# Hash attention and a gated feed-forward on one core: score masks of two blocks on quarters of TensorE's rows, score blocks and products with v by turns

## The chip, the core and the metric

The kernel runs on one core of a Trainium2 chip. The metric is the device time of one launch in microseconds (us). A core has TensorE (PE: matrix products, with its weight loads on their own row, PEld), VectorE (DVE), ScalarE (ACT), GpSimd (POOL) and SyncE (SP), which here only issues transfers. Each engine works through its own instructions in the order of the program and waits at an instruction until the semaphores that it names have been raised.

## The reference

```python
batch, n_heads, seq, head_dim = (4, 8, 768, 64)
q_bits = (np.einsum('bhsd,dk->bhsk', q, proj) > 0)      # 6 bits of each row
k_bits = (np.einsum('bhsd,dk->bhsk', k, proj) > 0)
mask = q_bucket[:, :, :, None] == k_bucket[:, :, None, :]
scores = scale * np.matmul(q, k.transpose(0, 1, 3, 2))
scores = np.where(mask, scores, -1000000000.0)
attn = softmax(scores)
x = np.matmul(attn, v)                # then (B,H,S,D) -> (B*S, H*D) = (3072, 512)
h = x @ w_in                          # 512 -> 2048
out = (h * erf(softplus(h))) @ w_out  # 2048 -> 512
```

A query attends only to the keys that have the same six bits.

## The kernel before, in words

The 32 heads are taken in 16 pairs. Two heads of 64 dimensions lie on the 128 partitions, one on the lower and one on the upper half (`ab` is 0 or 1 in the code). A pair has four groups n = 4 i to 4 i + 3: two halves of the queries (384 columns each), and for each half two groups of keys, of three blocks (c = 0, 1, 2) of 128 keys. So a half has 6 blocks, a pair 12, and attention 192.

`score` (line 730) computes one block, keys down and queries across, for both heads at once. Each head has its own bank of PSUM; a block takes one buffer `st` of two banks, and there are three such buffers. It is made in two steps. The mask step (source "b") is one bf16 product per head of the signs of the bits: `both` holds them, 64 rows per head, of which 7 are used (six bits and a constant) and the others are zero. It adds a very large negative number unless all bits agree. The plain step adds k times q in f32; an f32 product shows as two matmuls in the profile, so four for the two heads. Both steps use TensorE as two halves of 64 rows by 128 columns (the "64\*128" of a row in the profile).

ScalarE then takes the exponential of the block (`exponential`, line 772) into `e_even` or `e_odd`, one for each parity of the half; `e_odd` lies in the tile named `area`. VectorE adds up the exponentials of a pair (`sum_keys`, line 818). `weigh` (line 830) multiplies a group's three blocks with v; the two heads use two halves of TensorE's columns ("128\*64"), and the result of a half gathers in one bank, `av`. ScalarE copies it away (`leave`, line 895). The divisor is a product of the sums with ones on quarters of the columns ("128\*32", `divisor`, line 874); from there it goes through DRAM, is inverted on VectorE and comes back (`spread` to `normalise`, lines 914 to 957).

The bits of a pair are prepared ahead: TensorE multiplies q and k with the projection (`bits_of`, line 1033, "128\*32"), ScalarE takes the sign into `sg` (line 1042), VectorE scales it (line 1052), GpSimd writes it to DRAM (`leave_bits`, line 1062) and reads it back to its place in one of the two mask buffers (`place_bits`, line 1071, two transfers per pair). Pair 0's bits are made in place, without DRAM; its buffer is cleared afterwards (`clean`, line 1080).

Beside attention, the weights of the feed-forward are fetched by GpSimd and converted on ScalarE and VectorE (lines 651 to 727), 32 pieces.

TensorE's order in attention is a list written by hand (`order`): all 12 blocks of a pair (four entries "score"), then the products with v of all 12 (four entries "weigh"), then the bits of the pair after next and the divisor of the pair before. `pe(...)` gives each entry a cost and what it comes after; a score block must wait until the block that had its buffer three places ago has been taken by ScalarE. `arrange` then plays all engines forward with these costs and so sets the order of the other engines' instructions. The feed-forward follows (line 1493 on): TensorE begins it with products of the first tokens and w_in, for which VectorE has made sums of weights and tokens (lines 983 and 511) at the end of attention, and VectorE adds the first results up (line 1516).

Of the kernel before, what the change touches and what calls it, by code (L numbers as in the profile page):

```python
# [63 lines left out]
P = 128  # L64
# [288 lines left out]
def kernel(  # L353
# [11 lines left out]
    nc = tc.nc  # L365
# [241 lines left out]
    def attention():  # L607
        NS = NPAIR * 4
        with (
# [121 lines left out]
            def score(n, c, parts=((0, "b"), (1, ""))):  # L731

                i, half, g = n // 4, n // 2 % 2, n % 2
                d = pairs[i]
                cols = slice(half * HS, (half + 1) * HS)
                keys = slice((g * GC + c) * P, (g * GC + c + 1) * P)
                if ("st", n, c) in d:
                    parts = ((1, "b"),)
                else:
                    d["st", n, c] = big("st")  # L740
                st = d["st", n, c]
                for part, src in parts:
                    for ab in range(2):
                        rows = slice(ab * D, ab * D + D)
                        nc.tensor.matmul(  # L745
                            out=st[:, ab, 0:HS],
                            lhsT=d["k" + src][rows, keys],
                            rhs=d["q" + src][rows, cols],
                            start=(part == 0),
                            stop=(part == 1),  # L750
                        )

            def plain(n, c):
# [63 lines left out]
                        into, one, two = last_sums[:, 0, :, :], s[:, 0, 0, :, :], s[:, 0, 1, :, :]  # L817
                nc.vector.tensor_tensor(out=into, in0=one, in1=two, op=ALU.add)  # L818

            def weigh(n):  # L820
                half, g = n // 2 % 2, n % 2
                d = pairs[n // 4]
                if g == 0:
                    d["av", half] = bank("av") if half else psum_v.tile([P, 512], F32, name="av", tag="av")
                w = HS + 1 - half
                for c in range(GC):
                    e = block(n, c)
                    for ab in range(2):
                        rows = slice(ab * D, ab * D + D)
                        nc.tensor.matmul(  # L830
                            out=d["av", half][rows, 0:w],
                            lhsT=d["v"][:, g * GC + c, rows],
                            rhs=e[:, ab, 0:w],
                            start=(g == 0 and c == 0),
                            stop=(g == 1 and c == GC - 1),
                        )
# [227 lines left out]
            def place_bits(i):  # L1064

                d = pairs[i]
                bd = d.pop("bd")
                for n, what in enumerate(("qb", "kb")):
                    d[what] = both[i % 2][:, n, :]
                for ab in range(2):  # L1070
                    nc.gpsimd.dma_start(
                        out=both[i % 2][ab * D : ab * D + NBIT + 1, :, :].rearrange(
                            "r w (h c) -> r (w h) c", h=2
                        ),
                        in_=bd[:, ab, 0 : NBIT + 1, :].rearrange("n r c -> r n c"),
                    )

            def clean(n):

# [2 lines left out]
            chain = []  # L1082
            order = []
            PACE = 18
            for i in range(NPAIR):
                for k in range(4):
                    order.append(("score", 4 * i + k))
                    if i == 0 and k == 1:
                        order.append(("bits", 1))
                order += [("weigh", 4 * i + k) for k in range(4)]  # L1090
                if i + 2 < NPAIR:
                    order.append(("bits", i + 2))
                if 0 < i < NPAIR - 1:
                    order.append(("divisor", i - 1))
                if i == NPAIR - 2:
                    order.append(("divisor", i))
            slots = []
            for what, n in order:
                free = slots[-3] if len(slots) >= 3 else ()
                if what == "score":  # L1100
                    i = n // 4
                    after = (("place_bits", i),)
                    for c in range(GC):
                        free = slots[-3] if len(slots) >= 3 else ()
                        pe(score, (n, c), 0.82 if n or c == 2 else 0.17, after + free)
                        slots.append((("exponential", n, c),))
                elif what == "bits":
                    pe(bits_of, (n,), 0.80, (("start_pair", n),) + free)
                    slots.append((("sign_of", n),))
                elif what == "divisor":  # L1110
                    if n != NPAIR - 3:
                        free = ()
                        slots[-1] += (("keep_divisor", n),)
                    else:
                        slots.append((("keep_divisor", n),))
                    pe(divisor, (n,), 0.72, (("sum_keys", n, last_sum(n)),) + free)
                else:
                    h = n // 2
                    after = (("exponential", n, GC - 1),)
                    if n % 2 == 0:  # L1120
                        after += (("leave", h - 2), ("leave_plain", (h - 2) // 2))
                    pe(weigh, (n,), 2.0, after)
            sums_after = {}
            for i in range(NPAIR):
                for k, (_, blocks_) in enumerate(sum_steps(i)):
# [1543 lines left out]
```

## Time and profile before

| what | us |
|---|---|
| median of three timed runs | 866.1 (865.98 to 866.86) |
| the profiled execution, as timed | 866.67 |
| its span, first to last instruction | 864.9 |
| TensorE busy | 858.7 |
| VectorE busy | 728.2 |
| ScalarE busy | 636.5 |
| first feed-forward product begins | 312.84 |

The profile is of one execution; times in it count from its first instruction. In the timeline a row has the start, how long until the last of its instructions ended, engine, line, operation, what it writes and reads, the shape (for TensorE rows by columns of the array that are in use, then partitions by elements that stream), and how many instructions were merged into the row. Matmuls of TensorE overlap, so that the distance from start to start says what one costs, and the duration does not. In the rows that group instructions, the number behind the bar is busy time, and then the mean of one in ns.

### The profile page before, as it was taken

How to read it: one execution, taken by the hardware profiler on the slowest of the kernel's cores; microseconds unless marked ns; L12 is line 12 of the kernel's file. 1: busy time of each engine (PE TensorE's matmuls, PEld its weight loads, DVE VectorE, ACT ScalarE, POOL GpSimd, SP SyncE). 2: the span in 40 equal slices, each digit the busy share in tenths (PEclk: the TensorE clock that was granted, in tenths of full speed). 3: DMA queues.
4: the chain of work that ended last, by engine and by line, in shares of the span. 5: the costliest groups of instructions: out<-in, count | busy, mean ns of one | idle time of the engine just before them, and what ended most of it. 6: DMA issues, size and time to landing. Idle time of an engine off the chain costs nothing.

```text
span 864.9 us, 15750 instructions
## 1 busy us (share of the span) xinstructions
PE 858.7 (99%) x6184; PEld 672.6 (78%) x6184; DVE 728.2 (84%) x987; ACT 636.5 (74%) x890; POOL 179.5 (21%) x262
## 2 busy tenths in 40 slices
PE   9999999999999999999999999999999999999997
PEld 5444545444454468899999999999999999999997
DVE  5999999999999799778677999798879777967992
ACT  6888888888888759984689455876785768667840
POOL 1111111111111000233242334331321441110000
PEclk9999999999999999999999999999999999999999
DMA  9566876655663336497565658846667667555222
GB/s 224 155 177 196 212 213 166 192 149 149 185 170 111 102 130 220 144 357 270 184 167 181 222 174 249 280 150 217 176 226 267 208 219 203 207 184 176 75 69 70
DMA packets 103939, 160.57 MB, mean 186 GB/s; under 512 B 35646, under 2 KB 49006, under 8 KB 102960
## 3 DMA queue, kind: packets, MB, share of 16 engines
q1 hardware_dynamic: 94288, 126.47, 47.1%
q0 software_dynamic: 9120, 32.55, 11.9%
q8 instruction: 51, 0.84, 0.4%
q10 hardware_dynamic: 448, 0.46, 0.2%
q14 instruction: 32, 0.26, 0.1%
HBM read 125.01 MB, written 30.24 MB: 180 GB/s over the span
## 4 chain that ended last, share of the span: by engine, by line
PE 99%; DVE 1%; ACT 0%; issue 0%
PE M L1730 25%; PE st L745 18%; PE M L2038 18%; PE av L830 15%; PE M L2197 8%; PE X L2197 6%; PE M L1493 6%; PE bits L1033 1%; PE bits L874 1%; PE warm L994 1%; PE X L2038 0%; PE bits L564 0%; PE z_ps L874 0%; DVE h L1897 0%; DVE e L1897 0%; DVE w_out_sb L2123 0%
## 5 line engine op out<-in xcount | busy, mean ns | idle before, releaser
L1890 ACT ACTIVATE w<-w,cq 128x1024 f32<-128x1024 f32 x144 | 162.3, 1145 | 1.8
L745 PE MATMUL st<-q,k 64*128 64x384 f32 x768 | 155.1, 482 | 0.0
L1730 PE MATMUL M<-area,w_in_sb 128*128 128x128 f32 x1120 | 142.8, 275 | 0.0
L1760 DVE TENSOR_TENSOR h<-M,h 128x512 f32<-128x512 f32 x161 | 107.9, 685 | 37.4 <-PE M L1730 35.7
L1730 PEld LDWEIGHTS M<-area,w_in_sb 128*128 128x128 f32 x1120 | 137.2, 192 | 2.3
L1890 ACT ACTIVATE w<-h,cq 128x1024 f32<-128x1024 f32 x96 | 107.9, 1142 | 13.8 <-DVE e L1897 7.4
L2038 PE MATMUL M<-w_out_sb,h 128*128 128x256 f32 x464 | 109.9, 379 | 0.0
L1730 PE MATMUL M<-i,w_in_sb 128*128 128x128 f32 x840 | 107.4, 275 | 0.0
L1730 PEld LDWEIGHTS M<-i,w_in_sb 128*128 128x128 f32 x840 | 103.2, 192 | 1.8
L745 PEld LDWEIGHTS st<-q,k 64*128 64x128 f32 x768 | 68.5, 187 | 36.0 <-issue 34.6
L2038 PEld LDWEIGHTS M<-w_out_sb,h 128*128 128x128 f32 x464 | 83.9, 190 | 9.1
L818 DVE TENSOR_TENSOR area<-area 128x1536 f32<-128x1536 f32 (+1 forms) x46 | 79.1, 1720 | 7.0 <-ACT area L772 5.7
L1882 ACT ACTIVATE e<-h 128x1024 f32<-128x1024 f32 x48 | 50.5, 1053 | 37.2 <-DVE h L1760 30.8
L772 ACT ACTIVATE e_even<-st 128x768 f32<-128x768 f32 x96 | 73.9, 819 | 0.4 <-PE st L745 0.3
L1712 POOL TENSOR_TENSOR i<-area,i 128x128 f32<-128x128 f32 x70 | 41.6, 615 | 151.4 <-PE M L1730 150.6
L772 ACT ACTIVATE area<-st 128x768 f32<-128x768 f32 x90 | 72.7, 811 | 0.3 <-PE st L745 0.3
L1897 DVE SCALAR_TENSOR_TENSOR e<-w,e 128x1024 f32<-128x1024 f32 x48 | 61.3, 1279 | 13.2 <-ACT w L1890 13.1
L1897 DVE SCALAR_TENSOR_TENSOR h<-w,e 128x1024 f32<-128x1024 f32 x48 | 62.2, 1297 | 9.2 <-ACT w L1890 8.6
L830 PE MATMUL av<-e_even,v 128*64 128x385 f32 x384 | 65.7, 490 | 0.0
L745 PE MATMUL st<-both 64*128 64x384 bf16 x384 | 63.0, 323 | 0.2 <-ACT e_even L772 0.2
L830 PE MATMUL av<-area,v 128*64 128x384 f32 x360 | 60.6, 486 | 0.0
L2038 PE MATMUL M<-wt,area 128*128 128x256 f32 x224 | 55.8, 380 | 0.0
(203 smaller groups left out, 1368.8 us busy)
## 6 DMA issues: line engine op xcount, KB each, us to landing
w_in_sb<-wi_P SPq DMA_DIRECT2D x35, 1792.0 KB
raw<-in_w_out_dram POOLq DMA_DIRECT2D x16, 512.0 KB, 4.1
w_in_sb<-wm_M SPq DMA_DIRECT2D x30, 256.0 KB
raw<-in_w_in_dram POOLq DMA_DIRECT2D x14, 512.0 KB, 5.7
v<-in_v_dram SPq DMA_DIRECT2D x32, 192.0 KB
out_dram<-area SPq DMA_DIRECT2D x23, 256.0 KB
q<-in_qkT_dram SPq DMA_DIRECT2D x30, 192.0 KB
k<-in_qkT_dram SPq DMA_DIRECT2D x30, 192.0 KB
```

The costliest lines, as they stand in the source:

```text
L745: nc.tensor.matmul(out=st[:, ab, 0:HS], lhsT=d["k" + src][rows, keys], rhs=d["q" + src][rows, cols], start=(part == 0), stop=(part == 1),)
L772: nc.scalar.activation(out=e[:, :, 0:HS], in_=st[:, :, 0:HS], func=AF.Exp, scale=scale)
L818: nc.vector.tensor_tensor(out=into, in0=one, in1=two, op=ALU.add)
L830: nc.tensor.matmul(out=d["av", half][rows, 0:w], lhsT=d["v"][:, g * GC + c, rows], rhs=e[:, ab, 0:w], start=(g == 0 and c == 0), stop=(g = ...
L1493: nc.tensor.matmul(out=kept[where][:, u, :], lhsT=a[:, kc, f : f + P], rhs=b[:, kc, :], start=(first and u == 0 and kc == 0), stop=(end an ...
L1730: nc.tensor.matmul(out=out_[:, c, :], lhsT=ring[:, W_AT[q], n % 2, c * P : (c + 1) * P], rhs=x, start=((q in ("Q1", "Q5") or q == "Q2" and ...
L1760: nc.vector.tensor_tensor(out=out_, in0=bank_, in1=one, op=ALU.add)
L1882: nc.scalar.activation(out=s, in_=unit(t, q, fl), func=AF.Silu)
L1890: nc.scalar.activation(out=st["q", t, q, fl, j], in_=f, func=func, scale=scale, bias=cq[:, column : column + 1])
L1897: nc.vector.scalar_tensor_tensor(out=unit(t, q, fl) if last else s, in0=st.pop(("q", t, q, fl, j)), scalar=GATE_S[j][1], in1=s, op0=ALU.ad ...
L2038: nc.tensor.matmul(out=where[:, sub, :], lhsT=a[:, j // G, j % G, sub * P : (sub + 1) * P], rhs=b[:, j, :], start=first, stop=end, skip_gr ...
L2197: nc.tensor.matmul(out=where[:, n * P : n * P + P], lhsT=a[:, j, :], rhs=b[:, j, :], start=(q in ("Q1", "Q2") and j == 0), stop=(q in ("Q4 ...
```

## The change

It does five things.

1. A new function `masks` does the mask steps of two blocks together. Each head's bits are now held twice, in rows 0 to 6 and 32 to 38 of its 64; the first block uses the first quarter of TensorE's rows in each half, the second block the second. These are four bf16 matmuls of 32 rows by 128 columns. The plain steps of the two blocks follow. Pair 0 keeps the mask step of `score`.
2. `place_bits` places each head's bits twice: four transfers per pair instead of two.
3. The order on TensorE is made by halves: two score blocks, then two blocks' products with v of the half before, three times in each half. The first half has no products with v, and at the end those of the last half stand alone.
4. `weigh` takes some of a group's blocks at a time.
5. Bits of the pair after next follow the second half of a pair; the divisors of pairs 13 and 14 move behind the first half of pair 15.

```diff
                 if ("st", n, c) in d:
-                    parts = ((1, "b"),)
+                    parts = ((1, "b" if n == 0 and c < 2 else ""),)
...
+            def masks(*two):
+                i, half = two[0][0] // 4, two[0][0] // 2 % 2
+                d = pairs[i]
+                for n, c in two:
+                    d["st", n, c] = big("st")
+                for p, (n, c) in enumerate(two):
+                    keys = slice((n % 2 * GC + c) * P, (n % 2 * GC + c + 1) * P)
+                    for ab in range(2):
+                        rows = slice(ab * D + p * QR, ab * D + (p + 1) * QR)
+                        nc.tensor.matmul(
+                            out=d["st", n, c][:, ab, 0:HS],
+                            lhsT=d["kb"][rows, keys],
+                            rhs=d["qb"][rows, half * HS : (half + 1) * HS],
+                            start=True,
+                            stop=False,
+                        )
...
                 for ab in range(2):
-                    nc.gpsimd.dma_start(
-                        out=both[i % 2][ab * D : ab * D + NBIT + 1, :, :].rearrange(
...
+                    for row in (ab * D, ab * D + QR):
+                        nc.gpsimd.dma_start(
+                            out=both[i % 2][row : row + NBIT + 1, :, :].rearrange(
...
-            for i in range(NPAIR):
-                for k in range(4):
-                    order.append(("score", 4 * i + k))
...
-                order += [("weigh", 4 * i + k) for k in range(4)]
...
+            for h in range(NPAIR * 2 + 1):
+                i, half = divmod(h, 2)
+                scores = [(2 * h + g, c) for g in range(2) for c in range(GC)] if h < 2 * NPAIR else []
+                weighs = [(2 * h - 2 + g, c) for g in range(2) for c in range(GC)] if h else []
+                for k in range(GC):
+                    if scores:
+                        order.append(("masks" if i else "score", scores[2 * k : 2 * k + 2]))
+                    if weighs:
+                        order.append(("weigh", weighs[2 * k : 2 * k + 2]))
+                if h == 0:
+                    order.append(("bits", 1))
+                elif half and i + 2 < NPAIR:
                     order.append(("bits", i + 2))
-                if 0 < i < NPAIR - 1:
+                if half and 0 < i < NPAIR - 2:
                     order.append(("divisor", i - 1))
-                if i == NPAIR - 2:
-                    order.append(("divisor", i))
+                elif h == 2 * NPAIR - 2:
+                    order += [("divisor", i - 2), ("divisor", i - 1)]
...
-                        pe(score, (n, c), 0.82 if n or c == 2 else 0.17, after + free)
...
+                    if what == "masks":
+                        pe(masks, tuple(n), 0.17, after)
+                        for each in n:
+                            pe(score, each, 0.66)
```

In the rows below, a line of the order that stands for one matmul with f32 operands is two in the profile. TensorE before, the end of pair 1 (`both1` has its bits, `st_` and a number is one score buffer in use, `av_478` and `av_501` are the results of its two halves):

```order
L745 LDWEIGHTS both1_157
L745 MATMUL st_462<-both1_157 128x384
L745 MATMUL st_462<-q_204,k_205 128x384 x2
L745 LDWEIGHTS both1_157
L745 MATMUL st_471<-both1_157 128x384
L745 LDWEIGHTS both1_157
L745 MATMUL st_471<-both1_157 128x384
L745 MATMUL st_471<-q_204,k_205 128x384 x2
L830 MATMUL av_478<-e_even_159,v_206 64x385 x12
L830 MATMUL av_501<-area_76,v_206 64x384 x12
L1033 MATMUL bits_535<-q_379,proj_q_68 32x384 x2
```

TensorE now, in the second half of the same pair:

```order
L763 LDWEIGHTS both1_157
L763 MATMUL st_438<-both1_157 128x384
L763 LDWEIGHTS both1_157
L763 MATMUL st_438<-both1_157 128x384
L763 LDWEIGHTS both1_157
L763 MATMUL st_439<-both1_157 128x384
L763 LDWEIGHTS both1_157
L763 MATMUL st_439<-both1_157 128x384
L745 MATMUL st_438<-q_204,k_205 128x384 x2
L745 MATMUL st_439<-q_204,k_205 128x384 x2
L848 MATMUL av_460<-e_even_159,v_206 64x385 x4
L763 LDWEIGHTS both1_157
```

Each block's mask step stood ahead of its plain step; now both masks stand ahead of both plain steps, and four products with v of the half before (`e_even`) follow, ahead of the next masks.

GpSimd before, from the bits of pair 1 on (`bd` is their place in DRAM, `raw` a piece of weights):

```order
L1062 DMA bd_290<-sg_155 128x384
L1080 MEMSET both0_156 128x1536
L651 DMA raw_317<-in_w_in_dram 128x1024
L1071 DMA both1_157<-bd_290 7x4x384 x2
L651 DMA raw_372<-in_w_in_dram 128x1024
L1062 DMA bd_399<-sg_155 128x384
```

GpSimd now, at the same place:

```order
L1080 DMA bd_285<-sg_155 128x384
L651 DMA raw_315<-in_w_in_dram 128x1024
L1090 DMA both1_157<-bd_285 7x4x384 x4
L1099 MEMSET both0_156 128x1536
L1080 DMA bd_354<-sg_155 128x384
L651 DMA raw_383<-in_w_in_dram 128x1024
```

The transfers that place pair 1's bits are four, and the clearing of pair 0's mask buffer has moved from ahead of them to behind them.

More of the change, by code (lines that the diff above doesn't have):

```diff
@@ L818, in sum_keys, with weigh @@
                 nc.vector.tensor_tensor(out=into, in0=one, in1=two, op=ALU.add)
-            def weigh(n):
+            def weigh(n, some=()):
                 half, g = n // 2 % 2, n % 2
                 d = pairs[n // 4]
-                if g == 0:
+                if ("av", half) not in d:
                     d["av", half] = bank("av") if half else psum_v.tile([P, 512], F32, name="av", tag="av")
                 w = HS + 1 - half
-                for c in range(GC):
+                for c in some or (GC - 1,):
                     e = block(n, c)
@@ L1099, in attention @@
                 free = slots[-3] if len(slots) >= 3 else ()
[L1100 to L1104, printed above, removed]
-                        pe(score, (n, c), 0.82 if n or c == 2 else 0.17, after + free)
-                        slots.append((("exponential", n, c),))
+                if what in ("score", "masks"):
+                    after = (("place_bits", n[0][0] // 4),)
+                    for each in n:
+                        after += slots[-3] if len(slots) >= 3 else ()
+                        slots.append((("exponential",) + each,))
+                        if what == "score":
+                            pe(score, each, 0.82 if each[0] or each[1] == 2 else 0.17, after)
+                    if what == "masks":
+                        pe(masks, tuple(n), 0.17, after)
+                        for each in n:
+                            pe(score, each, 0.66)
                 elif what == "bits":
@@ L1117, in attention @@
                 else:
-                    h = n // 2
-                    after = (("exponential", n, GC - 1),)
-                    if n % 2 == 0:
+                    h = n[0][0] // 2
+                    after = (("exponential", 2 * h + 1, GC - 1),)
+                    if n[0] == (2 * h, 0):
                         after += (("leave", h - 2), ("leave_plain", (h - 2) // 2))
-                    pe(weigh, (n,), 2.0, after)
+                    for m, c in n:
+                        if c < GC - 1:
+                            pe(weigh, (m, (c,)), 0.66, after)
+                        else:
+                            pe(weigh, (m,), 0.66, after)
             sums_after = {}
```

11 lines of the change are left out of this document (4 added, 7 removed).

## The prediction

> **What bounds the kernel now.** I read the page first, then the busy time in stretches, then the timeline of TensorE through one pair of heads.
>
> ```profile
> span 864.9 us, 15750 instructions
> ...
> PE 858.7 (99%) x6184; PEld 672.6 (78%) x6184; DVE 728.2 (84%) x987; ACT 636.5 (74%) x890; POOL 179.5 (21%) x262
> ...
> PE 99%; DVE 1%; ACT 0%; issue 0%
> ```
>
> ```profile
> 100.00:200.00 100.00, 100.00 (x718) 48.08 (x716) 95.73 (x127) 83.87 (x147) 14.59 (x26) 1.00 0.66 179
> 200.00:300.00 100.00, 100.00 (x714) 48.34 (x712) 88.86 (x112) 83.91 (x144) 12.90 (x23) 1.00 0.49 137
> ```
>
> TensorE has no idle time in attention (columns: PE, PEld, DVE, ACT, POOL, then the granted clock, 1.00), and the chain that ended last is 99% TensorE. So whatever TensorE spends more or less, the span follows, until another engine has no time left. VectorE is the next candidate, at 95.73 of 100.
>
> But "busy" does not say that TensorE streams all that time. The timeline shows the spacing of starts:
>
> ```profile
> 103.04 0.83 PE L874 MATMUL bits<-area,ones 128*32 128x384 f32 x8
> 103.80 0.34 PE L745 MATMUL st<-both 64*128 64x384 bf16 x2
> 103.97 0.81 PE L745 MATMUL st<-q,k 64*128 64x384 f32 x4
> 104.62 0.33 PE L745 MATMUL st<-both 64*128 64x384 bf16 x2
> ...
> 112.69 0.33 PE L745 MATMUL st<-both 64*128 64x384 bf16 x2
> 112.85 0.81 PE L745 MATMUL st<-q,k 64*128 64x384 f32 x4
> 113.59 4.10 PE L830 MATMUL av<-e_even,v 128*64 128x385 f32 x24
> 117.53 4.04 PE L830 MATMUL av<-area,v 128*64 128x384 f32 x24
> 121.50 0.52 PE L1033 MATMUL bits<-q,proj_q 128*32 128x384 f32 x2
> ...
> 121.84 0.49 PE L1033 MATMUL bits<-q,proj_q 128*32 128x384 f32 x2
> ...
> 122.16 0.83 PE L874 MATMUL bits<-area,ones 128*32 128x384 f32 x8
> 122.92 0.34 PE L745 MATMUL st<-both 64*128 64x384 bf16 x2
> 123.10 0.81 PE L745 MATMUL st<-q,k 64*128 64x384 f32 x4
> 123.74 0.33 PE L745 MATMUL st<-both 64*128 64x384 bf16 x2
> ```
>
> A pair takes 122.92 - 103.80 = 19.12 us. One score block is its mask step (two bf16 matmuls side by side on 64 rows each, 112.85 - 112.69 = 0.16) and its plain step (four f32 matmuls, 0.645 to the next start, as from 103.97 to 104.62): 0.807. Twenty-four matmuls with v take 3.94, so four of them, one block, take about 0.65.
>
> Where the shape of the array changes (the "64*128" of a row: rows by columns), starts come later than the stream asks. From the last plain step to av: 113.59 - 112.85 = 0.74 instead of 0.645, 0.095 too late. From av to bits: 121.50 - 117.53 = 3.97 instead of 24 x 0.161 = 3.87, 0.10. From the sums by ones to a mask: 122.92 - 122.16 = 0.76 instead of two steps of 0.32, some 0.11. From bits to those sums the shape stays 128*32, although the sums wait for VectorE's semaphore, and the spacing stays at 0.32. So the pause goes with the shape and not with the waiting. Behind it the first matmul is also longer, since its weights were not loaded ahead:
>
> ```profile
> L830 PE MATMUL av<-e_even,v x24: 484/486/538, 113.6 to 117.2; 128*64 128x385 f32 x24
> L745 PE MATMUL st<-both x8: 322/323/333, 122.9 to 125.4; 64*128 64x384 bf16 x8
> L745 PE MATMUL st<-q,k x8: 482/482/587, 6.5 to 7.6; 64*128 64x384 f32 x8
> ```
>
> (min/median/max in ns.) That is 0.05 for the first av, 0.01 for the first bf16 mask, and 0.105 for a first f32 plain step; the last row is the one place, at 6.5 us, where plain steps come directly behind another shape.
>
> **The change, part by part.** The sum is against the profiled execution, 866.67 us; the median of the three timed runs is 866.1, 0.6 lower.
>
> *Masks of two blocks at once.* All but pair 0 use it: 180 of 192 blocks, 90 steps instead of 180. If four matmuls on 32 rows each stream side by side as two on 64 rows do, a step still takes 0.16, so 90 x 0.161 = 14.5 us go. The trace has four side by side only on columns (the sums by ones: eight matmuls of 384 columns in 0.83). At worst quarters stream two by two and nothing goes. I take 14.5, since the column quarters do stream together.
>
> *More changes of shape.* Per round (two blocks) TensorE now goes masks, plain, v, masks. There are 31 halves behind the first, with 3 rounds each: 93 steps of v, 90 of them with masks. Before there were 16 stretches of v. So the step from plain to v happens 93 - 16 = 77 times more often, at 0.095 + 0.05: 11.2 us. The step from v directly to a score did not exist; it comes 93 - 14 (bits follow) - 1 (divisors follow half 30) - 1 (feed-forward follows) = 77 times, at 0.10 + 0.01: 8.5 us. Changes around bits and divisors stay as many as before.
>
> *Masks to plain.* This step was free, both being 64*128. Now it goes from 32*128 to 64*128, which no row shows. From below: 0, if only a change of columns or of the full height pauses. From above: the pause 0.095 plus the first plain step's 0.105, 0.20. Every change of shape seen paused by about 0.1, also 128*64 to 128*32, where only the tile got smaller; I take 0.20: 90 x 0.20 = 18.0 us (bounds 0 to 18).
>
> The Trainium skill, "TensorEngine Tiling (Array Packing)", section Tiling Modes, says that changing the tiling mode, and not just the tile, drains TensorE, and it lists 64x128 and 32x128 as different modes. The trace agrees where columns change, with 0.095 us, and no row shows rows alone changing; by the rule alone, weights loaded ahead, the step would cost 90 x 0.095 = 8.6 us, by mine 18.0.
>
> *Pair 1's masks come earlier and their DMAs are twice as many.*
>
> ```profile
> 16.61 0.55 POOL L1062 DMA_DIRECT2D bd<-sg  x1 [14.03 <-DVE sg L1052]
> 23.39 1.14 POOL L1071 DMA_DIRECT2D both<-bd  x2 [3.53 <-DMA bd<-sg]
> both<-bd POOLq DMA_DIRECT2D x30, 21.0 KB, 2.5
> ```
>
> ```profile
> 13.57 0.34 PE L745 MATMUL st<-both 64*128 64x384 bf16 x2
> ...
> 27.21 0.34 PE L745 MATMUL st<-both 64*128 64x384 bf16 x2
> ```
>
> GpSimd cannot issue them before the bits have left, 23.39. Four instead of two, 0.57 each: the fourth starts at 25.1 and lands 2.1 to 2.5 later, at 27.2 to 27.6. Before, TensorE was there at 27.21. Now half 0's v comes between pair 0's later blocks and half 1's goes into pair 1: from 13.57 three rounds of 2 x 0.807 + 0.146 + 1.29 + 0.11 = 3.16, then the bits of pair 2, 0.77: 23.8. It waits 3.6 us (2 to 5), once; behind the waiting mask its whole queue stands. Later pairs have a pair's time for the same: lateness of 1.1 us in the fourth landing is covered by the other pair's 20 us. The clearing of the other mask buffer and a weight fetch move behind or ahead of these issues on GpSimd and cost TensorE nothing there.
>
> *Waits for free score buffers.* A pair of masks needs two of three. The later one is that of the block two back on TensorE, whose plain step ended 0.65 + 0.15 + 1.29 + 0.11 = 2.2 us earlier, and ScalarE needs about 0.2 + 0.82 for it:
>
> ```profile
> L772 ACT ACTIVATE e_even<-st 128x768 f32<-128x768 f32 x90 | 69.6, 819 | 0.4 <-PE st L745 0.3
> ```
>
> 1.2 us to spare hold one other operation of ScalarE (0.7). Cost 0; without that cover some 0.3 a round.
>
> *VectorE and ScalarE* keep their work: 95.73% and 83.87% of 19.12, that is 18.3 and 16.0 us a pair. They stay hidden as long as TensorE needs more than 18.3.
>
> *The end.* The sums of pair 15 now start behind the divisors of pair 13, which stand behind half 30, about 13.5 us ahead of feed-forward (three rounds and six blocks of v).
>
> ```profile
> 293.72 1.50 PE L874 MATMUL z_ps<-area,ones 128*32 128x384 f32 x16
> 312.84 5.45 PE L1493 MATMUL M<-area,w_in_sb 128*128 128x256 f32 x24
> 317.14 0.69 DVE L1594 TENSOR_TENSOR h<-w_in_sb,h 128x512 f32<-128x512 f32 x1
> 318.40 0.69 DVE L1516 TENSOR_TENSOR h<-M,h 128x512 f32<-128x512 f32 x1 [0.57 <-PE M L1493]
> ```
>
> Before it was 312.84 - 293.72 = 19.1 us. So VectorE enters feed-forward up to 5 us later than it did; it had 0.6 to spare at its first addition there, and TensorE's next use of these banks is some microseconds off. I take 0, with 0 to 4.
>
> *Sum:* -14.5 + 11.2 + 8.5 + 18.0 + 3.6 = +26.8. 866.67 + 26.8 = 893.5, and 0.6 less for a median: 893. A pair then takes about 19.12 - 0.97 + 6 x 0.20 + 5 x (0.146 + 0.11) = 20.6 us, and VectorE is at 89%.
>
> **The rivals.**
>
> *Rows alone don't pause* (chance 0.18). The step from masks to plain stays free, weights still loaded under the masks: 18.0 less, 875. For it: plain weights (64 rows) were always loaded under a running mask. Against: every change of shape on record paused. Between the two, pause without the weights' load: 884 (0.06).
>
> *The pause belongs to semaphores, not to shapes* (0.04 with its weaker form). Each pause on record stands where a matmul waits for another engine at a new stage. If that were the cause, the inner rounds, whose v steps mostly wait for nothing, would not pause: -14.5 + 3.6, bounded by VectorE's 18.3 us a pair instead of 17.8 while weights are converted, some +2: 858, faster than before. It decides if v follows plain without 0.095. Against: bits to sums waits and doesn't pause.
>
> *Quarters don't stream together* (0.06). Masks of two blocks take 0.32: 14.5 more, 908. The Trainium skill, "TensorE: Matmul & The Clock Gate", section Part 3, gives 3.07 times for four tiles of 32 rows, not four; by that a step would take 0.21, an estimate of 4 us more than mine. No run here shows it.
>
> *Waits in every round or at feed-forward's start* (0.06). ScalarE's order was planned for rounds of 2.8 us without pauses; if exponentials come behind two other operations, 0.1 to 0.2 us for each of 90 rounds: 902 to 911.
>
> **How the numbers follow.** The forecast, 893, has 0.60; its own range is 888 (stall 2, weights partly ahead) to 899 (stall 5, 4 at the end). The range 873 to 899 takes in the free step from masks to plain and leaves out the faster case, the quarters and the waits, 0.16. A measurement here can tell about 0.2%, 1.7 us, from no change. Faster 0.03 is the semaphore case; same 0.01 is kept for that case with its gain eaten by VectorE; all others are slower, 0.96.
>
> **What the changed profile would show.** Right: a masks step of four bf16 matmuls 0.16 to 0.18 long; 0.25 from its start to the first plain start and a first plain matmul of about 587 ns; v starting 0.74 behind the second plain step; a round of 3.2 us; a wait of TensorE near 24 us that a DMA of both ends. Wrong: plain 0.16 behind the masks with 482 ns throughout (875), v without pause (858), or idle TensorE in each round that ScalarE ends (above 899).

## The result, and the profile after

The changed kernel takes 900.6 us (median of four runs, 897.9 to 901.2) against 866.5 for the kernel before. The ratio is 1.0387, with a 95% interval of 1.0365 to 1.0410. The forecast was 893.0 with a range up to 899: the sign was right, the size 7.6 us short, and the time lies 1.6 us outside the range.

The first lines of the page, for the changed kernel's profiled execution (901.18 us as timed):

```profile
span 899.0 us, 15777 instructions
...
PE 887.6 (99%) x6184; PEld 655.2 (73%) x6184; DVE 730.6 (81%) x987; ACT 628.5 (70%) x890; POOL 197.2 (22%) x292
...
PE 93%; DVE 4%; ACT 1%; DMA 1%; issue 0%; POOL 0%; DVEq 0%
```

The span is 34.1 us longer (899.0 against 864.9). TensorE has as many instructions as before, 6184, but 29 us more busy time. And the chain that ended last has been 99% TensorE; now 7% of it runs over other engines and a DMA. So there are two kinds of loss, and the first product of the feed-forward separates them: it began at 312.84 and now begins at 342.98, 30.1 us later; from there to the end it was 552.0 us and is 556.0.

**The rounds.** TensorE's timeline in the middle of attention (start, duration, engine, line, operation, shape, count):

```profile
102.07 0.34 PE L763 MATMUL st<-both 32*128 32x384 bf16 x4
102.34 1.56 PE L745 MATMUL st<-q,k 64*128 64x384 f32 x8
103.83 1.51 PE L848 MATMUL av<-e_even,v 128*64 128x385 f32 x8
105.28 0.34 PE L763 MATMUL st<-both 32*128 32x384 bf16 x4
...
111.70 0.52 PE L1051 MATMUL bits<-q,proj_q 128*32 128x384 f32 x2
...
132.37 0.52 PE L1051 MATMUL bits<-q,proj_q 128*32 128x384 f32 x2
```

A round is 105.28 - 102.07 = 3.21 us, and a pair, from one set of bits to the next, 132.37 - 111.70 = 20.67. Forecast were 3.2 and 20.6. The masks of two blocks take 0.27 to the next start, and no row of this stretch shows TensorE idle. The durations of single matmuls (minimum, median and maximum in ns) in this same round, plain steps and then products with v:

```profile
L745 PE MATMUL st<-q,k x8: 482/482/587, 102.3 to 103.4; 64*128 64x384 f32 x8
L848 PE MATMUL av<-e_even,v x8: 484/487/538, 103.8 to 104.9; 128*64 128x385 f32 x8
```

587 ns for the first plain matmul and 538 for the first with v are the late weights, 0.105 and 0.05. They come in every round: from 100 to 200 us the mean of the plain matmuls is 508 ns, that is 482 and a quarter of 105, one late matmul in four.

The busy time in stretches (PE, PEld, DVE, ACT, POOL, then the granted clock) shows that no other engine has become the bound: VectorE went from 95.73 to 83.47.

```profile
100.00:200.00 100.00, 100.00 (x662) 38.93 (x660) 83.47 (x109) 75.87 (x134) 17.44 (x31) 1.00 0.60 164
```

**Pair 1's start.** The timeline of TensorE from the bits of pair 2 on (in brackets the idle time ahead of a row and what ended it):

```profile
23.64 0.49 PE L1051 MATMUL bits<-k,proj_q 128*32 128x384 f32 x2
25.78 0.33 PE L763 MATMUL st<-both 32*128 32x384 bf16 x1 [1.64 <-DMA both<-bd]
26.89 0.34 PE L763 MATMUL st<-both 32*128 32x384 bf16 x2 [0.78 <-DMA both<-bd]
27.43 0.49 PE L763 MATMUL st<-both 32*128 32x384 bf16 x1 [0.20 <-DMA both<-bd]
27.85 2.93 PE L745 MATMUL st<-q,k 64*128 64x384 f32 x8
30.71 2.83 PE L848 MATMUL av<-area,v 128*64 128x384 f32 x8
33.47 0.51 PE L763 MATMUL st<-both 32*128 32x384 bf16 x4
33.91 1.56 PE L745 MATMUL st<-q,k 64*128 64x384 f32 x8
```

The wait is there: without it the masks would have begun at 24.06 (the last bits' start, 23.64, and 0.42 to the next shape), and the last of the four begins at 27.43, 3.4 us later. But what follows is new: the eight matmuls of two plain steps take from 27.85 to 30.71, 2.86 us, where 1.49 is usual (102.34 to 103.83), and the products with v 2.76 instead of 1.45. The stretches say why:

```profile
26.00:27.00 1.00, 0.22 (x3) 0.09 (x2) 1.00 (x1) 0.55 (x2) 1.00 (x1) 1.00 0.17 43
27.00:28.00 1.00, 0.80 (x5) 0.25 (x3) 0.97 (x2) 0.00 (x0) 0.59 (x2) 0.55 0.00 0
28.00:30.00 2.00, 2.00 (x8) 1.03 (x8) 1.97 (x3) 0.45 (x1) 0.25 (x1) 0.50 0.14 49
...
33.00:34.00 1.00, 1.00 (x8) 0.20 (x6) 0.97 (x2) 0.00 (x0) 0.15 (x1) 0.53 0.94 354
34.00:36.00 2.00, 2.00 (x12) 0.94 (x14) 0.28 (x1) 1.13 (x2) 0.43 (x1) 1.00 0.77 161
```

The granted clock was halved. If it has only the values 1.00 and 0.50, a mean of 0.55 in the slice from 27 means low for 0.90 of it, and 0.53 in the one from 33 low for 0.94: from 27.10 to 33.94, 6.84 us. TensorE had work from 27.43 on. From there to the plain steps at 33.91 it took 6.48 us, where the same steps in the round above take 3.21 + 0.27 = 3.48: 3.0 us lost, a little less than half, since the eight plain matmuls and the eight with v did not quite double.

The four timed executions bear this out. Three have a mean granted clock of 0.995 and take 900.4 to 901.2 us; one has 1.000 and takes 897.9, that is 2.5 to 3.3 us less, and lies inside the forecast's range. So the wait does not lower the clock in every execution of this kernel.

**The feed-forward's start.** TensorE in the changed kernel:

```profile
342.98 5.45 PE L1525 MATMUL M<-area,w_in_sb 128*128 128x256 f32 x24
348.35 0.84 PE L892 MATMUL X<-area,ones 128*32 128x384 f32 x4
350.28 0.84 PE L892 MATMUL X<-area,ones 128*32 128x384 f32 x4 [1.09 <-DVE area L836]
...
372.16 3.72 PE L1525 MATMUL M<-area,w_in_sb 128*128 128x256 f32 x16 [1.50 <-ACT h L1538]
...
376.30 3.72 PE L1525 MATMUL M<-area,w_in_sb 128*128 128x256 f32 x16 [0.41 <-ACT M L1541]
```

The divisor of pair 15 (`X`, L892) waits for VectorE's sums of that pair; some 22 us on TensorE waits again, for ScalarE's copies of results. In the kernel before, neither place waits:

```profile
318.22 0.85 PE L874 MATMUL X<-area,ones 128*32 128x384 f32 x8
...
338.40 7.17 PE L1493 MATMUL M<-area,w_in_sb 128*128 128x256 f32 x32
```

Compared matmul by matmul with that kernel, each counted from the feed-forward's first product, TensorE is 1.9 us late behind the first of these places, 3.6 behind the second, 4.2 behind the third. VectorE's timeline at that place, first before the change, then after:

```profile
305.81 0.90 DVE L818 TENSOR_TENSOR area<-q,k 128x768 f32<-128x768 f32 x1
```


```profile
329.00 1.76 DVE L836 TENSOR_TENSOR area<-e_even 128x1536 f32<-128x1536 f32 x1 [0.62 <-PE z_ps L892]
...
339.73 0.16 DVE L919 TENSOR_SCALAR ev<-av 128x1 f32<-128x1 f32 x1 [1.38 <-ACT x_last L913]
...
345.30 0.95 DVE L836 TENSOR_TENSOR area<-q,k 128x768 f32<-128x768 f32 x1
```

The sums of pair 15 (L836) begin at 329.00, but the pieces that the second half of that divisor needs begin only at 345.30, 2.3 us behind the feed-forward's first product; before, they began 7.0 us ahead of it. They stand behind the copy of a column of `av` (L919), which waits for ScalarE, behind inversions, and behind sums for the feed-forward.

So the account of the span's 34.1 us has three parts: the forecast's rounds (-14.5 + 11.2 + 8.5 + 18.0 = 23.2; 15 pairs at 20.67 instead of 19.12 are 23.3) and the wait (3.4), a low clock (3.0), and the feed-forward's start (4.0): 33.6. Of the 0.5 left, 0.2 lies ahead of all this: the mask step behind the bits of pair 1 begins at 13.79 instead of 13.57, with TensorE's order still the same. The low clock and the feed-forward's start still needed proof.

### The profile page after: what moved, and what is told of

Read it like the earlier page. It is cut to its first block, busy times and chain, and to the rows that moved or that the text cites. A ratio compares the mean times of both kernels' runs of the same rounds, so it can differ in the third digit from the quotient of the medians.

```text
span 899.0 us, 15777 instructions
## 1 busy us (share of the span) xinstructions
PE 887.6 (99%) x6184; PEld 655.2 (73%) x6184; DVE 730.6 (81%) x987; ACT 628.5 (70%) x890; POOL 197.2 (22%) x292
## 4 chain that ended last, share of the span: by engine, by line
PE 93%; DVE 4%; ACT 1%; DMA 1%; issue 0%; POOL 0%; DVEq 0%
PE M L1762 24%; PE M L2070 17%; PE st L745 15%; PE av L848 15%; PE M L2229 8%; PE X L2229 6%; PE st L763 3%; PE M L1525 2%; PE bits L1051 1%; PE bits L892 1%; DVE area L836 1%; DMA bd<-sg 1%; ACT w L1922 1%; DVE h L1626 1%; PE warm L1012 1%
## 5 line engine op out<-in xcount | busy, mean ns | idle before, releaser
L745 PE MATMUL st<-q,k 64*128 64x384 f32 x768 | 151.5, 511 | 0.0
L745 PEld LDWEIGHTS st<-q,k 64*128 64x128 f32 x768 | 66.7, 187 | 41.7 <-issue 18.3
L836 DVE TENSOR_TENSOR area<-area 128x1536 f32<-128x1536 f32 (+1 forms) x46 | 79.9, 1738 | 13.3 <-ACT area L790 12.7
L790 ACT ACTIVATE area<-st 128x768 f32<-128x768 f32 x90 | 68.4, 808 | 31.3 <-PE st L745 31.2
L848 PE MATMUL av<-e_even,v 128*64 128x385 f32 x384 | 72.7, 499 | 0.0
L848 PE MATMUL av<-area,v 128*64 128x384 f32 x360 | 69.3, 507 | 0.0
L848 PEld LDWEIGHTS av<-e_even,v 128*64 128x64 f32 x384 | 23.3, 136 | 43.4 <-issue 35.8
```

The lines of the kernel that those rows point to most:

```text
L745: nc.tensor.matmul(out=st[:, ab, 0:HS], lhsT=d["k" + src][rows, keys], rhs=d["q" + src][rows, cols], start=(part == 0), stop=(part == 1),)
L790: nc.scalar.activation(out=e[:, :, 0:HS], in_=st[:, :, 0:HS], func=AF.Exp, scale=scale)
L848: nc.tensor.matmul(out=d["av", half][rows, 0:w], lhsT=d["v"][:, g * GC + c, rows], rhs=e[:, ab, 0:w], start=(g == 0 and c == 0), stop=(g = ...
```

## The experiments

The theory: each round costs what the forecast said, the rest is a low clock after idle time, and an order of VectorE that was planned for a shorter round than TensorE has. The rivals stand with each run. "Begins" is the feed-forward's first product, "from there" the time to the end of the span. In these traces the mask step behind the bits of pair 1, up to which TensorE's order is the same in all, begins between 12.95 us (the last row of the table) and 13.79 (the changed kernel), and at 14.76 with half the exponentials; differences of "begins" carry these differences too.

| kernel | median us | ratio to before, 95% | begins | from there |
|---|---|---|---|---|
| before | 866.5 | | 312.8 | 552.0 |
| changed | 900.6 | 1.0387 (1.0365 to 1.0410) | 343.0 | 556.0 |
| turns only | 892.1 | 1.0295 (1.0278 to 1.0312) | 335.9 | 554.1 |
| packed masks only | 905.6 | 1.0453 (1.0436 to 1.0471) | 351.2 | 552.0 |
| the same, half the exponentials | 884.0 | 1.0206 (1.0189 to 1.0223) | 329.2 | 551.9 |
| v blocks ahead | 898.2 | 1.0365 (1.0348 to 1.0382) | 337.0 | 560.5 |
| divisors earlier | 902.2 | 1.0416 (1.0399 to 1.0433) | 342.2 | 558.0 |
| 24 products in the wait | 899.6 | 1.0383 (1.0366 to 1.0400) | 341.6 | 556.1 |
| 14 products in the wait | 898.2 | 1.0372 (1.0354 to 1.0389) | 339.7 | 556.0 |
| true costs | 896.9 | 1.0342 (1.0325 to 1.0359) | 342.4 | 552.7 |
| true costs, v blocks ahead | 892.4 | 1.0301 (1.0279 to 1.0324) | 337.5 | 553.4 |
| turns only, true costs, v ahead | 886.3 | 1.0234 (1.0217 to 1.0251) | 331.2 | 553.1 |

### Turns only

The changed order with each block's own mask step on 64 rows, and two transfers for a pair's bits:

```diff
-                    for row in (ab * D, ab * D + QR):
+                    for row in (ab * D,):
...
-                        order.append(("masks" if i else "score", scores[2 * k : 2 * k + 2]))
+                        order.append(("score", scores[2 * k : 2 * k + 2]))
```

> The new order with each block's own mask step on 64 rows again, and two transfers for a pair's bits. Theory (each change of the array's shape pauses TensorE, rows included): a round is 3.16 us instead of the changed kernel's 3.21, 4.2 us less over 90 rounds, and the wait ahead of pair 1's masks is about 1.3 us shorter: 895 us, or 892 if the low clock behind that wait goes with it. Rival (packing the masks pays and only the turns cost): taking the packing back adds up to 14.5 us to 900.6: 915.

It took 892.1, and the rival's 915 is out. That this is the theory's second figure is in part luck: the low clock did not go, it became shorter, and the feed-forward's start lost 2.0 us where it had lost 4.0, which the theory did not have. The packed masks, with their change of shape, thus cost 8.5 us on top of the turns and save nothing: some 4 of them in the rounds (3.21 for 3.16), the rest by a longer wait, a longer low clock and the feed-forward's start. The timeline of TensorE in this run, and the plain steps' durations:

```profile
101.10 0.34 PE L745 MATMUL st<-both 64*128 64x384 bf16 x2
101.28 0.81 PE L745 MATMUL st<-q,k 64*128 64x384 f32 x4
```

```profile
L745 PE MATMUL st<-q,k x8: 482/482/483, 101.3 to 102.4; 64*128 64x384 f32 x8
```

From masks to plain on the same 64 rows no plain matmul is longer than 483 ns; behind masks on 32 rows the first took 587. The loads of the plain step's weights begin within the row of loads at 101.10 here, beside the masks, and in the changed kernel at 102.34, behind them. So a change of the rows alone keeps the weights' load from going ahead, 0.105, and makes a pause, 0.09: from 101.10 to 101.28 is 0.18, and the changed kernel's step from 102.07 to 102.34 is 0.27. The clock fell here too, after a wait of 2.1 us in which TensorE was idle for 1.55 and 0.18, and for half as long; the stretches:

```profile
25.00:26.00 1.00, 0.76 (x4) 0.51 (x6) 0.94 (x3) 0.88 (x4) 0.57 (x2) 0.92 0.00 0
26.00:29.00 3.00, 3.00 (x12) 1.36 (x10) 2.93 (x5) 1.05 (x2) 1.17 (x3) 0.50 0.10 33
29.00:30.00 1.00, 1.00 (x8) 0.28 (x4) 0.90 (x2) 1.00 (x2) 0.88 (x2) 0.88 0.84 102
```

Low for 0.16 of the first, all of the second and 0.24 of the third: 3.40 us. From the second mask, at 25.57, to the next round's masks, at 30.37, are 4.80 us where 3.16 is usual: 1.6 lost. Here too one execution of four has a higher mean clock than the others, 0.999 against 0.996.

### Packed masks only

The old order of whole pairs, with the packed masks:

```diff
-            for h in range(NPAIR * 2 + 1):
...
+            for i in range(NPAIR):
+                each = [(4 * i + g, c) for g in range(4) for c in range(GC)]
+                for k in range(6):
+                    order.append(("masks" if i else "score", each[2 * k : 2 * k + 2]))
...
+                order += [("weigh", each[2 * k : 2 * k + 2]) for k in range(6)]
```

> The masks of two blocks at once, but in the order of before: all 12 blocks of a pair, then all products with v. Theory: per pair 6 x 0.20 (masks to plain) + 5 x 0.105 (plain to masks) - 0.97 (six mask steps fewer) = +0.76 us, 15 pairs: +11.4, and 0.4 of wait ahead of pair 1's masks: 878 us; no plain step behind masks begins earlier than 0.25 us. Rival (rows alone cost little, the turns make the loss): 14.5 us less than before at best, bounded by ScalarE's 0.82 a block: 860 to 866.

It took 905.6: both expectations missed, the theory's by 27 us, and the feed-forward's start was as in the kernel before (552.0), which clears the packed masks of those waits. Here is what was overlooked, in TensorE's timeline and then ScalarE's:

```profile
118.42 1.56 PE L745 MATMUL st<-q,k 64*128 64x384 f32 x8
119.91 0.67 PE L763 MATMUL st<-both 32*128 32x384 bf16 x4
120.51 1.56 PE L745 MATMUL st<-q,k 64*128 64x384 f32 x8
```

```profile
119.38 1.51 ACT L790 ACTIVATE e_even<-st 128x768 f32<-128x768 f32 x2
```

The masks take 0.60 to the next start instead of 0.27, and a round of score blocks 120.51 - 118.42 = 2.09 instead of the expected 1.76. With three buffers, the second block of a round of masks needs the buffer of the first block of the round before. For the masks at 119.91 that is the block whose plain step began at 118.42; its exponential is the first of the two from 119.38 on, and runs about 0.8. So the buffer comes free near 120.2, and 120.2 plus 0.27 is 120.5, where the plain steps begin. Masks of two blocks at once need two free buffers of three, and without products with v between them the wait for ScalarE stands open: 0.33 each, the "some 0.3 a round" that the prediction named as the price without that cover.

### Half of the exponentials

The same, with ScalarE taking the exponential of half of the columns; the other half is a constant:

```diff
+            nc.gpsimd.memset(e_even[:, :, :, HS // 2 : HS], 1.0)
+            nc.gpsimd.memset(e_odd[:, :, :, HS // 2 : HS], 1.0)
...
+                part = HS if n >= NS - 2 else HS // 2
...
-                    out=e[:, :, 0:HS], in_=st[:, :, 0:HS], func=AF.Exp, scale=scale
+                    out=e[:, :, 0:part], in_=st[:, :, 0:part], func=AF.Exp, scale=scale
```

> Packed masks in the old order of pairs, with ScalarE's exponential over half of each block's columns (the other half is a constant set at the start, so half of the exponentials are left out; the last two groups are whole). Theory, what made the packed masks alone 905.6 is their wait for a score buffer that ScalarE's exponential still reads: with ScalarE ahead the round is 1.76 us (masks 0.16, a pause of 0.10 and its weights' load 0.10, two score blocks 1.40), and the time 878 or a little less. Rival, the 905.6 belongs to the packed masks themselves (their quarters or their second bank): about 905 with any ScalarE.

884.0: 21.6 of the 27.6 us above 878 are gone, and the round is as expected in TensorE's timeline (its line numbers are two higher, for the two lines added):

```profile
114.18 0.35 PE L765 MATMUL st<-both 32*128 32x384 bf16 x4
114.46 1.56 PE L747 MATMUL st<-q,k 64*128 64x384 f32 x8
115.95 0.35 PE L765 MATMUL st<-both 32*128 32x384 bf16 x4
```

115.95 - 114.18 = 1.77, with the masks at 0.28. The wait for ScalarE was the cause. Of the 6 us left, part is the constant itself: the first plain step of the launch begins 1.2 us later than in the kernel before (7.69 against 6.49; from 5.87 to 6.71 in the other runs). In about half of the pairs one wait of 0.33 is left, so that pairs take 19.96 or 20.28 us. The rest was not traced.

### The wait filled with products

TensorE multiplies ones by ones between the bits of pair 2 and pair 1's masks; 24 products first, then 14:

```diff
+            def fill(n):
+                scratch = bank("scratch")
+                for _ in range(24):
+                    nc.tensor.matmul(
+                        out=scratch[0:D, 0:P],
+                        lhsT=ones,
+                        rhs=ones[:, 0:1].broadcast_to([P, P]),
...
+                    if h == 1:
+                        order.append(("fill", 0))
```

> The changed kernel with 24 small float products (ones by ones, 64x128, into the scratch bank) on TensorE between the bits of pair 2 and pair 1's masks, so that TensorE works while both is on its way. Theory, idle time lowers the clock: pair 1's masks still begin near 27.5 us, but the granted clock stays at 1.00 from 24 to 34 us where the changed kernel shows 0.89 and 0.51; 2.8 us less than the changed kernel's 900.6, so 897.8. Rival, the low clock belongs to the mask products or the transfers and not to the waiting: the clock falls all the same, 900.6.

899.6, between the two: the clock stayed at 1.00, but the 48 matmuls ran until 29.05, 1.6 us past the landing, and gave about half of the saving back. With fewer:

```diff
-                for _ in range(24):
+                for _ in range(14):
```

> The run with small products in the wait again, with 14 of them for 24: 28 passes of 0.115 us are 3.2 us, which end near 26.8 and so ahead of the landing of both (the 24 ended at 29.05, some 1.6 us behind it, and gave back most of what the clock had saved). Theory, idle time lowers the clock: masks begin near 27.5 as in the changed kernel, the clock stays at 1.00 to 34 us, the feed-forward begins near 340.2 instead of 342.98, and the whole takes 897.8. Rival, the saving of the 24 had another cause: 899.6 or more.

898.2, 2.4 less by the medians; in the profile the feed-forward begins at 339.70, 3.3 us earlier than in the changed kernel, of which 0.4 lies ahead of the wait (TensorE comes to it at 23.69 instead of 24.06). The timeline of TensorE and the stretches of this run:

```profile
23.69 3.32 PE L841 MATMUL scratch<-ones 128*64 128x128 f32 x28
26.95 0.56 PE L763 MATMUL st<-both 32*128 32x384 bf16 x4
27.44 1.56 PE L745 MATMUL st<-q,k 64*128 64x384 f32 x8
```

```profile
24.00:28.00 4.00, 4.00 (x36) 3.40 (x35) 3.94 (x3) 2.14 (x6) 3.59 (x5) 1.00 0.08 22
28.00:34.00 6.00, 6.00 (x42) 2.27 (x40) 5.72 (x10) 5.17 (x9) 3.27 (x7) 1.00 0.51 145
```

Same masks, same transfers, and the plain steps run at full speed; in all eight executions of these two kernels the mean granted clock is 0.999 or 1.000. So it is idle time of TensorE that lowered the clock, not the masks or the transfers. The size, 2.9 here, agrees with the 3.0 worked out above and with the 2.8 that the expectations took from the doubled durations of one round.

### V blocks ahead, divisors earlier

Two attempts to take the stalls out by the order alone. First, the products with v of pair 0's second half stand ahead of pair 1's masks:

```diff
+                if h == 2:
+                    order += [("weigh", weighs[2 * k : 2 * k + 2]) for k in range(GC)]
+                    weighs = []
```

> The changed kernel, but the products with v of pair 0's second half stand ahead of pair 1's masks, where TensorE waits. Theory (the idle time lowers the granted clock behind it): the wait of about 3.5 us is filled, the granted clock stays at 1.0 from 20 to 40 us, and some 0.6 us of changes of shape fall away: 900.6 - 3.5 - 2.8 - 0.6 = 894 us. Rival (the low clock belongs to the mask steps or to the transfers): the clock falls all the same, 896.5.

The feed-forward begins at 337.03, 5.95 earlier (0.7 of it ahead of the wait, 13.11 against 13.79), and the clock stays at 1.00 from 20 to 44 us; but from there on it takes 560.5, 4.4 more than in the changed kernel. In TensorE's timeline:

```profile
347.40 1.49 PE L892 MATMUL X<-area,ones 128*32 128x384 f32 x4 [4.15 <-DVE area L836]
```

The second half of `X` could start 2.9 us earlier than in the changed kernel (350.28), but TensorE was there 6 us earlier: it waited 4.15 us for the sums, and after that idle time the clock was low once more, 0.50 from 347 to 352. Second, the divisors of pairs 13 and 14 behind the second round of half 30, for VectorE to start on pair 15's sums earlier:

```diff
+                    if h == 2 * NPAIR - 2 and k == 1:
+                        order += [("divisor", i - 2), ("divisor", i - 1)]
...
-                elif h == 2 * NPAIR - 2:
-                    order += [("divisor", i - 2), ("divisor", i - 1)]
```

> The changed kernel, but the divisors of pairs 13 and 14 stand one round earlier, behind the second round of half 30, which lets VectorE begin the sums of pair 15 about 3 us earlier. Theory (4 us of waits at the feed-forward's start come from VectorE's late sums): 1.5 to 3 us less than the changed kernel, 897.6 to 899, and the wait between the two parts of the last divisor (1.1 us) gone. Rival (VectorE has no time to gain, or the waits are ScalarE's own): 900.6 unchanged.

A miss: 902.2, and 558.0 from the feed-forward's start. VectorE's planned order had put normalising steps ahead of the sums, and `X` waited 3.70 us for them. So an earlier place of the divisors alone does not make the sums earlier; what VectorE's written order puts ahead of them does more. The next run goes at that order itself.

### True costs

TensorE's order stays; the planner is told what the steps take, pauses included:

```diff
-                        pe(masks, tuple(n), 0.17, after)
-                        for each in n:
-                            pe(score, each, 0.66)
+                        pe(masks, tuple(n), 0.28, after)
+                        for k, each in enumerate(n):
+                            pe(score, each, 0.65 if k else 0.85)
...
-                            pe(weigh, (m, (c,)), 0.66, after)
+                            pe(weigh, (m, (c,)), 0.65 if k else 0.79, after)
```

> The changed kernel, with the planner told what the steps take in its trace, pauses included: masks 0.28, the first score block of a round 0.85 and the second 0.65, the first block with v 0.79 and the second 0.65 (3.22 us a round for 2.81). TensorE's order of blocks is the same; VectorE's written order follows the later TensorE. Theory, the 4.0 us that the feed-forward takes longer are waits for sums of pair 15 that stand too late in VectorE's order, since the planner took TensorE to be earlier than it is: the time from the feed-forward's first product to the end of the span falls from 556.05 to about 552, and the whole to 896.6. Rival, they come from the new order of blocks itself (the divisors of pairs 13 and 14 behind the last half), whatever VectorE's order: 900.6.

896.9, with 552.7 from the feed-forward's start: 3.3 of the 4.0 us are gone, as the theory had it, and the rival falls. VectorE's timeline, then TensorE's:

```profile
336.41 0.95 DVE L836 TENSOR_TENSOR area<-q,k 128x768 f32<-128x768 f32 x1
...
339.13 0.16 DVE L919 TENSOR_SCALAR ev<-av 128x1 f32<-128x1 f32 x1 [1.13 <-ACT x_last L913]
...
344.72 0.95 DVE L836 TENSOR_TENSOR area<-area,v 128x768 f32<-128x768 f32 x1
```

```profile
342.38 5.45 PE L1525 MATMUL M<-area,w_in_sb 128*128 128x256 f32 x24
347.75 0.85 PE L892 MATMUL X<-area,ones 128*32 128x384 f32 x8
```

The sums start ahead of the step that waits (336.41 instead of 345.30) and end at 345.7; all eight matmuls of `X` run in one row without a wait, and the later waits for ScalarE's copies are gone with it. Then these costs together with the v blocks ahead:

```diff
+                if h == 2:
+                    order += [("weigh", weighs[2 * k : 2 * k + 2]) for k in range(GC)]
+                    weighs = []
...
-                        pe(masks, tuple(n), 0.17, after)
+                        pe(masks, tuple(n), 0.28, after)
```

> Both at once: the planner told the true lengths, and the products with v of pair 0's second half put ahead of pair 1's masks. Theory, the wait ahead of pair 1's masks with its low clock (6.0 us) and the waits at the feed-forward (4.0) are apart from each other: the feed-forward begins near 337.0 as with the v blocks ahead alone, takes about 552, and the whole is 890.7. Rival, the v blocks ahead take TensorE's lead over VectorE away, and the wait for the sums comes back at the feed-forward whatever the planner knows, as in the run with the v blocks ahead (560.5): 898.

892.4, with 337.51 and 553.4: the losses are apart from each other, and the rival's 898 is out. 1.7 us more than expected, of which 0.5 is the start and 1.4 the feed-forward, not traced further.

### Turns only, with both mends

The last kernel, with each block's own masks instead of the packed ones:

```diff
-                    for row in (ab * D, ab * D + QR):
+                    for row in (ab * D,):
...
-                        order.append(("masks" if i else "score", scores[2 * k : 2 * k + 2]))
+                        order.append(("score", scores[2 * k : 2 * k + 2]))
...
-                            pe(score, each, 0.82 if each[0] or each[1] == 2 else 0.17, after)
+                            pe(score, each, 0.86 if each[0] or each[1] == 2 else 0.17, after)
```

> The turns without the packed masks (each block's own 64-row masks), with the planner told the lengths with pauses and the products with v of pair 0's second half ahead of pair 1's masks. Theory, three losses of the turns are apart from each other: the wait with its low clock (feed-forward begins about 3 us earlier than the 335.85 of the turns only, 332.9), and the late sums (from there 552.3 instead of 554.08); the pauses of the turns stay, 77 times 0.255 less what they save at the old borders. The whole 887.2. Rival, the v blocks ahead bring the wait for the sums back: 891 or more.

886.3. The feed-forward begins 4.6 us earlier than with the turns only, where 3 were expected: the wait there had cost 2.1 and the low clock 1.6, and v blocks in one stretch save two turns each way (0.5), which the expectation left out. It is the fastest order by turns that was tried and is 20 us slower than the kernel before: what is left are the pauses of the turns. No experiment points to a version that beats the kernel before.

## Why the prediction fell short, point by point

- **Packed masks save 14.5: right.** From masks to plain steps is 0.27 us by the rows (102.07 to 102.34), against 0.18 for two matmuls on 64 rows (101.10 to 101.28). The 0.09 between is what a change of shape takes, as from plain to v: 1.49 (102.34 to 103.83) is four spacings of 0.322, the 0.105 of the weights, and 0.095. Nothing is left over for quarters that stream two by two, 0.32 alone; that rival (908) falls. How the 0.27 divides into streaming and pause is worked out from the other pauses, and no run shows it by itself: a step of 0.21, as in the prediction's estimate, with a pause of 0.06 would look the same.
- **Changes of shape, 11.2 + 8.5: right.** The spacings, the first v matmul of 538 ns and the rounds of the turns only (3.16) carry them. No row of the inner rounds shows TensorE waiting, and v pauses all the same; so the semaphores' rival (858) falls.
- **Masks to plain, 18.0: right, at its upper bound.** Both halves of it were seen, the pause and the 587 ns. The rivals at 875 and 884 fall. The Trainium skill, "TensorEngine Tiling (Array Packing)", section Tiling Modes, says that a change of mode drains TensorE; the trace agrees for rows too, with 0.09 us. The other 0.105, of weights that no longer load under the matmul before, is not in that rule, and 8.6 us by the rule alone would have been some 9 too few.
- **"It waits 3.6 us (2 to 5), once": right as a wait, incomplete as a cost.** It was 3.4. The step took idle time to cost its own length and looked at the queue behind it, not at the clock after it. Another 3.0 us went at half the clock, in three executions of four, and filling the wait brought 2.9 back. This is the step that put the time outside the range: 893 with 4.0 more for the end is 897, inside it, and so is the one execution without the low clock, 897.9. The Trainium skill, "TensorE: Matmul & The Clock Gate", Part 1, says that the clock halves after about one idle window of 3.4 us and comes back after a busy one. The trace agrees in the length, 3.40 us in one run and 6.84, twice that, in the changed kernel. It does not agree in the condition: with the turns only 1.7 us of idle time in two pieces were enough.
- **"The end ... I take 0, with 0 to 4": wrong.** It was 4.0. The prediction saw that VectorE would enter the feed-forward up to 5 us later, and took the slack of TensorE's banks for cover. What failed is the cover, and the place: VectorE's first addition there began 9.0 us behind the feed-forward's first product (352.00) instead of 2.4 (315.21), 6.6 later, and TensorE waited first not for those banks but, in `X`, for the sums of pair 15. The reason is the planner, whose costs make a round 0.17 + 4 x 0.66 = 2.81 us, while TensorE's takes 3.21, so VectorE's order was written for a TensorE that is early, with a step that waits ahead of the sums which TensorE then waits for; with true costs 3.3 of the 4.0 went. The rival "waits in every round or at feed-forward's start" had the right place, with 0.06, for its second half.
- **Score buffers, 0: right**, and the run without products with v between the rounds measured what they hide.
- **VectorE and ScalarE hidden: right** in the rounds (VectorE at 83% where 89% was forecast), wrong in the last 20 us.

The range ended at 899 since it took the upper ends of the wait and of the end as the worst; the low clock was in neither.

## What to carry to other kernels

Count every change of TensorE's shape, rows included, as a price per turn (here 0.10 us and the first weights' load), and set it against what packing saves (here 0.16 per round against 0.20 for masks to plain alone, and 0.46 with the turns to and from v). A wait of TensorE can cost nearly as much again in the clock behind it, unless something keeps TensorE busy: here waits of 2.1 and 3.4 us cost 1.6 and 3.0 more. And when a planner writes the order of other engines, give it measured step times: wrong ones move the loss to the place where the next stage begins.

## What the runs showed of the hardware that was not expected

The granted clock went low in pieces of about 3.4 or 6.8 us. It was low for one piece where TensorE's waits were over when the clock fell (turns only, 3.40; divisors earlier, 3.4), and for two where it still waited then (the changed kernel, idle until 27.43 with the clock low from 27.10; v blocks ahead, idle until 347.40 with the clock low from 346.0). Waits of 1.09 and 1.50 us at the feed-forward's start, in the changed kernel, did not lower it; 1.55 and 0.18 us close together, with the turns only, did. Nor did the same wait lower it each time: one execution of four of the changed kernel had a mean clock of 1.000 where the others had 0.995, and one of the turns only 0.999 where the others had 0.996. What decides between these was not tried.
